# Sixty-four unread bytes behind the attention's output: every feed-forward tile starts 64 bytes later

## The chip, the cores and the metric

One core of one Trainium2 chip runs the whole program. The metric is the device time of one execution in microseconds (us). It is given as the median of three runs, and one more execution was recorded by the hardware profiler.

## What is computed

A decaying linear attention is followed by two feed-forward layers, on 4 x 768 = 3,072 tokens of 256 channels. Cut to what matters:

```python
# attention, per batch and head (8 heads of 32 channels, 16 states), chunk by chunk
y[:, :, sl] = M @ xc + (Cc @ state) * decay_to_i      # M = (Cc Bc^T) * decays, causal
state = decay_full * state + sum_j(Bc_j x_j * decay_from_j)
# first feed-forward layer, d_ff = 1024
xk = mu_k * x + (1 - mu_k) * x_prev ; xr = mu_r * x + (1 - mu_r) * x_prev
k = max(xk @ w_k, 0) ; r = sigmoid(xr @ w_r) ; x = r * ((k * k) @ w_v)
# second feed-forward layer, d_ff = 2048
h = x @ w_in ; out = (h - tanh(h)) @ w_out
```

## The kernel before, in words

Channels lie on the 128 partitions, in two halves, and tokens run along the free dimension, in 6 blocks of 512. The attention's output and, later, the first layer's output are kept in one tile, `xall`, two halves of `NTOK + 8` float32 a partition. A program written out by hand, and then a planner with due times (`Plan.run`), set the order in which every engine's instructions stand.

Each float32 matrix product is made of three float32r matmuls on TensorE: a number is split into a high and a low part, and weight-high x data-high, weight-low x data-high and weight-high x data-low are added in PSUM. The function `product` (L755, L756, L758) does this for the products whose sums go up (into `pk`, `pr` in the first layer, `ph` in the second), and `down_part` (L765, L766, L767) for those that go down into `acc`. Every one of these matmuls has a 128x128 weight block, 512 contiguous bytes a partition, and streams 512 columns of data, 2,048 contiguous bytes a partition. Before each there is a weight load of its own (LDWEIGHTS).

A block of the first layer takes 108 such matmuls, 648 in all. The second layer is cut into 48 units (6 blocks, j, times 8 slices of 256 hidden channels, i); a unit takes 12 matmuls up and 12 down. Between the two ScalarE squares the result twice (`poly_a`, L884 and L885), VectorE finishes a polynomial for h - tanh(h) (L889, L893), one of the two copies the high part (L352 or L354), and VectorE makes the low part (L902). Six buffers serve in turn: `xh` and `xl` hold a block's data, `h` and `l` a unit's result, both streamed by TensorE; `f` and `s` are for ScalarE and VectorE.

Where the tiles stand follows from the order in which pools are opened. From the low end of each partition come the constants, `xall` (pool `zp`), the buffers `f h s l xh xl` (pool `work`), the second layer's weights of units i = 0 and 1 (pool `w2e`) and all weights of the first layer (pool `w1p`). From the high end comes a right-hand side: the attention's tiles (pool `att`), and after it, in the same place, the second layer's weights of units i = 2 to 7 (pool `w2p`) and the output buffers `ob`. In the built program, in bytes of each partition:

| tiles | start before | modulo 128 | start after | modulo 128 |
|---|---|---|---|---|
| `xall`, first half | 2,912 | 96 | 2,912 | 96 |
| `xall`, second half | 15,232 | 0 | 15,264 | 32 |
| `f h s l xh xl` (4,096 bytes each) | 27,552 and on | 32 | 27,616 and on | 96 |
| `winh winl wouth woutl`, i = 0, 1 (2,048 each) | 88,992 and on | 32 | 89,056 and on | 96 |
| `wkh wkl wrh wrl wvh wvl` | 105,376 and on | 32 | 105,440 and on | 96 |
| attention's `sr` (weights of `pd`), `rr` (its data) | 163,808 and 164,832 | 96 | the same | 96 |
| `winh winl wouth woutl`, i = 2 to 7 | 159,712 and on | 96 | the same | 96 |

All tiles of the first four kinds that TensorE reads have lengths that are multiples of 512 bytes, so that a weight block or a half of a data tile has the remainder of its tile. The matmul of L428, whose result is `pd`, is one of the attention's: 116 rows of weights from `sr`, 512 columns of `rr`, two in a row, placed between matmuls of the first layer.

Of the kernel before, what the change touches and what calls it, by code (L numbers as in the profile page):

```python
# [7 lines left out]
F32 = mybir.dt.float32  # L8
# [8 lines left out]
P = 128  # L17
# [3 lines left out]
NTOK = NB * S  # L21
# [174 lines left out]
def chain_kernel(ctx, tc, xb, a, an, a0, bc, mu_k, mu_r, w_k, w_v, w_r, w_in, w_out, out):  # L196
# [7 lines left out]
    zp = ctx.enter_context(tc.tile_pool(name="zp", bufs=1))  # L204
# [37 lines left out]

    xall = zp.tile([P, 2, NTOK + 8], F32, name="xall")

    def col(t):
        return t + t // S
# [856 lines left out]
```

## Time and profile before

| | |
|---|---|
| median of 3 runs | 507.31 us (507.01 to 508.74) |
| the profiled execution | 507.41 us, its span 505.7 us |
| TensorE busy | 482.5 us, 95% of the span |
| TensorE weight loads | 382.3 us, 76% |
| VectorE busy | 401.4 us, 79% |
| ScalarE busy | 293.1 us, 58% |
| mean granted TensorE clock | 0.978 |

The span runs from the first to the last instruction. TensorE's matmuls overlap in the profile and their ends are modelled, so that the busy share says that it always had one in flight, not how fast they followed each other; that is read from their starts.

### The profile page before, as it was taken

Reading aid. Unit: us, or ns where it says so; the run is one execution under the profiler, and the core shown is the slowest. Engines: PE = TensorE matmul, PEld = TensorE weight load, DVE = VectorE, ACT = ScalarE, POOL = GpSimd, SP = SyncE. Lnnn points to the kernel's source line nnn. Section 1 sums busy time; section 2 is a strip of 40 time slices with the busy share of each in tenths; the row PEclk is TensorE's granted clock in tenths of the full one; section 3 lists DMA queues with packets and bytes.
Section 4 is the critical chain, followed back from the end, with each engine's and each line's share of the span. In section 5 each row is a group of like instructions: output and inputs, shape, how many; then the busy total and the mean of one; then the engine's idle time right before and its main releaser. Section 6 shows DMA issues by size and latency. Waiting matters only on the chain.

```text
span 505.7 us, 10270 instructions
## 1 busy us (share of the span) xinstructions
PE 482.5 (95%) x4462; PEld 382.3 (76%) x4462; DVE 401.4 (79%) x509; ACT 293.1 (58%) x374; POOL 6.1 (1%) x22
## 2 busy tenths in 40 slices
PE   5979989999999999999999999999999999999993
PEld 2557767888778878877788788788878888887882
DVE  6698998999669999996877868767876966787581
ACT  5366976775757666766464654645565454455551
POOL 4000000000000000000000000000000000000000
PEclk9789999999999999999999999999999999999998
DMA  6575455211022212210000100100010010001001
GB/s 196 183 231 181 136 156 152 76 47 34 1 86 84 83 43 84 83 43 0 1 0 1 41 0 1 41 3 0 1 41 0 1 41 1 0 1 41 0 2 47
DMA packets 14259, 27.40 MB, mean 54 GB/s; under 512 B 2392, under 2 KB 3288, under 8 KB 14208
## 3 DMA queue, kind: packets, MB, share of 16 engines
q1 hardware_dynamic: 14140, 26.66, 16.9%
q8 instruction: 37, 0.61, 0.5%
q14 instruction: 14, 0.11, 0.1%
q10 hardware_dynamic: 68, 0.02, 0.0%
HBM read 23.30 MB, written 3.34 MB: 53 GB/s over the span
## 4 chain that ended last, share of the span: by engine, by line
PE 69%; DVE 18%; ACT 6%; DMA 3%; issue 2%; ACTq 0%; POOL 0%; DVEq 0%; POOLq 0%; SPq 0%
PE acc L765 10%; PE acc L767 10%; PE acc L766 10%; PE ph L755 8%; PE ph L758 8%; PE ph L756 8%; PE pk L755 3%; PE pk L756 2%; PE pk L758 2%; DVE l L788 2%; DVE f L889 2%; DVE f L893 1%; DMA raw<-in_w_in 1%; PE py L504 1%; PE py L482 1%
## 5 line engine op out<-in xcount | busy, mean ns | idle before, releaser
L884 ACT ACTIVATE s<-ph 128x1024 f32<-128x1024 f32 (+1 forms) x49 | 49.4, 1009 | 76.3 <-PE ph L758 76.3
L889 DVE SCALAR_TENSOR_TENSOR f<-f,s 128x1024 f32<-128x1024 f32 (+1 forms) x49 | 58.8, 1200 | 34.8 <-ACT f L885 34.4
L755 PE MATMUL ph<-xh,winh 128*128 128x512 f32 x192 | 76.2, 397 | 0.0
L756 PE MATMUL ph<-xh,winl 128*128 128x512 f32 x192 | 75.5, 393 | 0.0
L765 PE MATMUL acc<-h,wouth 128*128 128x512 f32 x188 | 74.5, 396 | 0.2
L767 PE MATMUL acc<-l,wouth 128*128 128x512 f32 x188 | 74.5, 396 | 0.1
L766 PE MATMUL acc<-h,woutl 128*128 128x512 f32 x188 | 74.3, 395 | 0.0
L902 DVE TENSOR_TENSOR l<-f,h 128x1024 fp32r<-128x1024 f32 (+1 forms) x49 | 58.9, 1201 | 18.6 <-ACT h L352 18.0
L352 ACT ACTIVATE h<-f 128x1024 fp32r<-128x1024 f32 (+1 forms) x43 | 44.7, 1039 | 48.5 <-DVE f L893 45.6
L893 DVE TENSOR_TENSOR f<-ph,f 128x1024 f32<-128x1024 f32 (+1 forms) x49 | 58.9, 1201 | 3.3
L758 PE MATMUL ph<-xl,winh 128*128 128x512 f32 x192 | 60.2, 395 | 0.0
L885 ACT ACTIVATE f<-s,biases 128x1024 f32<-128x1024 f32 (+1 forms) x49 | 55.6, 1136 | 1.6
L765 PEld LDWEIGHTS acc<-h,wouth 128*128 128x128 f32 x188 | 35.4, 188 | 10.0 <-ACT f L885 1.4
L755 PEld LDWEIGHTS ph<-xh,winh 128*128 128x128 f32 x192 | 36.1, 188 | 8.8
L758 PEld LDWEIGHTS ph<-xl,winh 128*128 128x128 f32 x192 | 36.1, 188 | 8.6
L767 PEld LDWEIGHTS acc<-l,wouth 128*128 128x128 f32 x188 | 35.4, 188 | 9.2 <-DVE l L902 1.0
L756 PEld LDWEIGHTS ph<-xh,winl 128*128 128x128 f32 x192 | 36.1, 188 | 8.1
L766 PEld LDWEIGHTS acc<-h,woutl 128*128 128x128 f32 x188 | 35.4, 188 | 8.2
L755 PE MATMUL pk<-xh,wkh 128*128 128x512 f32 x96 | 39.3, 409 | 0.0
L765 PE MATMUL acc<-h,wvh 128*128 128x512 f32 x96 | 38.5, 401 | 0.9 <-DVE xall L817 0.9
L756 PE MATMUL pk<-xh,wkl 128*128 128x512 f32 x96 | 38.2, 398 | 0.0
L767 PE MATMUL acc<-l,wvh 128*128 128x512 f32 x96 | 37.6, 392 | 0.3 <-DVE l L788 0.3
(138 smaller groups left out, 754.0 us busy)
## 6 DMA issues: line engine op xcount, KB each, us to landing
bct<-in_bc SPq DMA_DIRECT2D x12, 384.0 KB
xbt<-in_xb SPq DMA_DIRECT2D x12, 384.0 KB
raw<-in_w_in SPq DMA_DIRECT2D x8, 512.0 KB
raw<-in_w_out SPq DMA_DIRECT2D x8, 512.0 KB
out<-ob SPq DMA_DIRECT2D x11, 256.0 KB
raw<-in_w_k SPq DMA_DIRECT2D x4, 512.0 KB
raw<-in_w_v SPq DMA_DIRECT2D x4, 512.0 KB
raw<-in_w_r SPq DMA_DIRECT2D x1, 512.0 KB
```

What stands on the lines that cost most here:

```text
L352: A.activation(out=out, in_=in_, func=AF.Copy)
L755: PE.matmul(o, wh[:, k, ms], hi[:, k], start=k == 0, stop=False)
L756: PE.matmul(o, wl[:, k, ms], hi[:, k], start=False, stop=False)
L758: PE.matmul(o, wh[:, k, ms], lo[:, k], start=False, stop=k == 1)
L765: PE.matmul(acc[:, c], wh[:, k, cs], h[:, e], start=first, stop=False, skip_group_check=True)
L766: PE.matmul(acc[:, c], wl[:, k, cs], h[:, e], start=False, stop=False, skip_group_check=True)
L767: PE.matmul(acc[:, c], wh[:, k, cs], l[:, e], start=False, stop=last, skip_group_check=True)
L884: A.activation(out=s, in_=phs[j, i][:, e], func=AF.Square, accum_out=sums[:, c:c + 1])
L885: A.activation(out=qs[j, i][:, e], in_=s, func=AF.Square, scale=PA, bias=pbias)
L889: V.scalar_tensor_tensor(out=q, in0=q, scalar=PG, in1=s, op0=ALU.add, op1=ALU.mult)
L893: V.tensor_tensor(out=q, in0=phs[j, i][:, e], in1=q, op=ALU.mult)
L902: V.tensor_tensor(out=l[:, e], in0=qs[j, i][:, e], in1=f(h[:, e]), op=ALU.subtract)
```

## The change

The tile `xall` gets 16 columns more than tokens in each half in place of 8. Nothing reads or writes the new columns.

```diff
-    xall = zp.tile([P, 2, NTOK + 8], F32, name="xall")
+    xall = zp.tile([P, 2, NTOK + 16], F32, name="xall")
```

The tile grows by 2 x 8 x 4 = 64 bytes a partition. Its second half moves by 32 bytes, and all that is allocated after it from the low end moves by 64, as in the table. The right-hand side stays where it was. Every engine's instructions are the same, in the same order; only addresses differ.

## Rows read from the trace of the kernel before

**Rows 1.** The page: shares by engine of the chain of work that ended last.

```profile
PE 69%; DVE 18%; ACT 6%; DMA 3%; issue 2%; ACTq 0%; POOL 0%; DVEq 0%; POOLq 0%; SPq 0%
```

**Rows 2.** The chain that ended last, in order of time: start, length, what.

```profile
474.06 0.48 PE ph L758 x2
474.57 1.12 ACT s L884 x2
...
495.19 3.02 PE acc L972 x18
```

**Rows 3.** The waits that began from 242 to 474 us: total, times, longest.

```profile
ACT s L884 <- PE ph L758: 67.0, 40, 3.3
...
PEld acc L765 <- ACT f L885: 1.4, 3, 0.5
```

**Rows 4.** TensorE in order of time, first layer: start, length, line, tiles.

```profile
191.18 0.39 PE L755 MATMUL pk<-xh,wkh 128*128 128x512 f32 x1
...
193.90 0.39 PE L755 MATMUL pk<-xh,wkh 128*128 128x512 f32 x1
```

**Rows 5.** The same view, second layer, units i = 3 to 7 of j = 1.

```profile
299.14 0.40 PE L755 MATMUL ph<-xh,winh 128*128 128x512 f32 x1
...
303.34 0.40 PE L765 MATMUL acc<-h,wouth 128*128 128x512 f32 x1
...
304.74 0.40 PE L755 MATMUL ph<-xh,winh 128*128 128x512 f32 x1
```

**Rows 6.** Stretches side by side: TensorE busy (instructions), granted clock, DMA share, GB/s.

```profile
145.00:223.00 78.00, 77.14 (x344) 1.00 0.27 82
242.00:474.00 232.00, 231.77 (x993) 1.00 0.03 12
```

**Rows 7.** The same for all engines: PE, PEld, DVE, ACT, POOL, then clock.

```profile
190.00:218.00 28.00, 28.00 (x125) 23.10 (x125) 27.26 (x39) 20.57 (x24) 0.00 (x0) 1.00 0.31 93
300.00:328.00 28.00, 28.00 (x122) 22.51 (x121) 22.92 (x23) 14.50 (x20) 0.00 (x0) 1.00 0.05 19
```

**Rows 8.** TensorE in order of time, j = 5: units i = 0 between others.

```profile
445.96 0.39 PE L767 MATMUL acc<-l,wouth 128*128 128x512 f32 x1
...
447.58 0.39 PE L755 MATMUL ph<-xh,winh 128*128 128x512 f32 x1
...
448.94 0.40 PE L765 MATMUL acc<-h,wouth 128*128 128x512 f32 x1
...
450.33 0.39 PE L755 MATMUL ph<-xh,winh 128*128 128x512 f32 x1
```

**Rows 9.** Weight loads in order of time, beside the matmuls of Rows 5.

```profile
303.34 0.19 PEld L766 LDWEIGHTS acc<-h,woutl 128*128 128x128 f32 x1
```

**Rows 10.** TensorE in order of time around two pairs of `pd`.

```profile
61.07 0.62 PE L428 MATMUL pd<-rr,sr 116*128 116x512 f32 x2
61.52 0.39 PE L755 MATMUL pr<-xh,wrh 128*128 128x512 f32 x1
...
105.37 0.62 PE L428 MATMUL pd<-rr,sr 116*128 116x512 f32 x2
105.82 0.39 PE L765 MATMUL acc<-h,wvh 128*128 128x512 f32 x1
```

**Rows 11.** TensorE in order of time where block 5 takes over `acc`.

```profile
459.64 0.63 PE L758 MATMUL ph<-xl,winh 128*128 128x512 f32 x2
...
460.65 0.39 PE L766 MATMUL acc<-h,woutl 128*128 128x512 f32 x1
```

**Rows 12.** Two lines that read both halves of `xall`: ns min/median/max.

```profile
L775 ACT ACTIVATE f<-xall,muk x12: 711/716/723, 34.6 to 182.2; 128x512 f32<-128x512 f32 x12
...
L780 DVE SCALAR_TENSOR_TENSOR f<-xall,omk,f x12: 743/746/751, 35.4 to 184.9; 128x512 f32<-128x512 f32 x12
```

**Rows 13.** VectorE's writes into weight tiles, by line: busy, mean ns of one.

```profile
L329 DVE TENSOR_TENSOR winl<-keep,winh 128x512 fp32r<-128x512 f32 x8 | 5.5, 686 | 0.1
L329 DVE TENSOR_TENSOR wkl<-keep,wkh 128x512 fp32r<-128x512 f32 x4 | 2.7, 687 | 0.9 <-ACT wkh L352 0.9
```

## The prediction

> **What bounds the kernel now.** The question is whether 64 bytes of address can matter at all, so the views are read in this order: the chain that ended last, to see whose speed sets the end; the waits, to see whether that engine is held up by others; and then the starts of its instructions, to see what its speed depends on.
>
> The chain lies on TensorE for 69% of the span [rows 1]. In the second layer it stays there from 242 to 474 us; the last 31 us belong to ScalarE and VectorE, which work off the last units, and TensorE's last 18 matmuls [rows 2]. In those 232 us ScalarE waits 67.0 us for TensorE, while the largest of the waits of TensorE's weight loads is 1.4 us in all [rows 3]. So from 242 to 474 us a nanosecond saved on a matmul is a nanosecond of the end, and elsewhere only in part.
>
> The starts tell the speed. In the first layer 12 matmuls start between 191.18 and 193.90: 2.72 us / 12 = 226.7 ns each [rows 4]. In the second layer 24 start between 299.14 and 304.74: 5.60 / 24 = 233.3 ns [rows 5]. The matmuls are of one form, 128x128 by 512 columns of float32r, and both stretches have the full granted clock, 1.00 [rows 6, 7]. The other engines are not the reason either: VectorE is busy 27.26 of 28 us where the matmuls are fast, and 22.92 of 28 where they are slow; ScalarE 20.57 and 14.50 [rows 7].
>
> What differs is the address. In the first layer data and weights both start at 32 modulo 128 (the table of tiles). In rows 5 the data start at 32 and the weights, of units i = 3 to 7, at 96. The second layer has its own test of this, since units i = 0 and 1 have weights at 32. In block 5 unit 0 comes up between units whose weights are at 96: from 445.96 to 447.58 seven matmuls take 1.62 / 7 = 231.4 ns, the next six, to 448.94, take 1.36 / 6 = 226.7 ns, and the six that follow, with weights at 96 again, 1.39 / 6 = 231.7 ns [rows 8]. Within 5 us, with the same clock and the same company, the slow pace goes when the remainders agree and comes back when they do not. That it takes some matmuls to settle suggests a phase: the weights of a matmul are read while the data of the one before stream (the load for L766 starts at 303.34 with the matmul of L765, and ends 0.19 us later [rows 5, 9]), and the two reads get out of each other's way only if their lines agree. This is a conjecture; the pace is what is measured.
>
> **The change, part by part.** No instruction is added, removed or moved.
>
> *Data tiles and first-layer weights go from 32 to 96 together.* Their distance stays a multiple of 128 (of 512, even). If distance counts, the first layer keeps its 226.7 ns. The trace has one matmul with both operands at 96: `pd`. Its pairs stand among first-layer matmuls, and where these are settled the pair takes 0.45 us, from 61.07 to 61.52 and from 105.37 to 105.82, so 225 ns each [rows 10]. That is the fast pace, with weights at 96. It has 116 rows instead of 128, and a pair is short, so this speaks for the distance without proving it.
>
> *Second-layer weights of units 2 to 7 stay at 96, and the data come to them.* Distance 64 becomes 0. The price of a matmul afterwards is bounded by the two paces of the trace, 226.7 below and 233.3 above; I take 226.7, since rows 4, 8 and 10 all show it wherever the remainders agree. Between 242 and 474 us there are 993 matmuls [rows 6]: 993 x 226.7 ns = 225.1 us in place of 232.0. From the difference of 6.9 us come off the halts of TensorE that remain, where a block's `acc` is waited for: the three matmuls from 459.64 to 460.65 take 1.01 us in place of 0.70, 0.31 us lost [rows 11]. There are three like this and some smaller ones, 1.0 us by my estimate. A halt waits for ScalarE's copy while TensorE has less to do meanwhile, so each of the five block ends grows by about 6 matmuls x 6.6 ns = 0.04 us, 0.2 us. After each some matmuls are unsettled again, 7 x (231.4 - 226.7) ns = 0.03 us [rows 8], 0.2 us in all. 6.9 - 1.0 - 0.2 - 0.2 = 5.5 us.
>
> *Before 242 and after 474 us* I count nothing: there ScalarE, VectorE and their transfers hold the chain. That the attention's `pd`, now at the same remainder as its neighbours, disturbs them less could give up to 0.5 us; it widens the range only.
>
> *Does the faster TensorE run into another engine?* A unit takes 24 x 233.3 = 5.60 us now and would take 5.44. ScalarE waits 67.0 us for TensorE in 232 us [rows 3], 28 us per 100, so it can follow a pace that is 2.8% faster. What is late next is the low part `l` (L902), for which the weight load of L767 waits; TensorE has waited little for it so far, and it would have some 0.25 us less (an estimate: about 40 matmuls x 6.6 ns lie between the release of ScalarE's first square and that load).
>
> *`xall`'s second half moves from 0 to 32 modulo 128; every buffer and first-layer weight tile of ScalarE and VectorE moves too.* L775 and L780 read both halves, which stand 32 apart modulo 128, in 711 to 723 and 743 to 751 ns [rows 12]; L329 writes `wkl` at 32 in 687 ns and `winl`, mostly at 96, in 686 [rows 13]. Those engines do not care: 0 us. If they did by the whole spread of rows 12, 1%, it would be hidden where TensorE bounds.
>
> A rule of the Trainium skill speaks against all this. "SBUF — State Buffer", section "Who interferes with whom", gives TensorE two independent read ports, one for the moving operand and one for LDWEIGHTS, and says that PE and ACT never wait on anyone. By that, no address would change the pace and the sum would be 0 us. The trace does not agree: 226.7 and 233.3 ns in rows 4, 5 and 8 with nothing else changed.
>
> Sum: -5.5 us on the profiled execution's 507.41 us (its span, 505.7, and 1.7 around it, which stays) gives **501.9 us**. That execution is 0.1 us above the median shown, 507.31, which the range covers.
>
> **The rivals.**
>
> *The weights' own address counts (slower).* If a weight block at 96 is slow by itself, whatever the data's address, the change makes slow what was fast. The first layer's 648 matmuls lose 6.6 ns each, of which the 344 from 145 to 223 us [rows 6] fully (2.3 us), and the 304 before, where the attention is interleaved, between nothing and all (up to 2.0 us). In the second layer units 0 and 1 lose about 233.3 - 229.2 (13 matmuls of rows 8 in 2.98 us) = 4 ns on some 250 matmuls, 1.0 us. Sum +3.3 to +5.3, middle 511.7 us. For it: in rows 4, 5 and 8 a weight at 96 always goes with 233 ns, since the data never moved. Against it: `pd` [rows 10]. The point that decides is the first layer's pace: above about 229 ns with all at 96, this is it.
>
> *The remainder is not the cause (no change), 507.4 us.* The weights that go with 233.3 ns also lie above byte 157,000 of the partition, those with 226.7 below 142,240 (105,376 + 4 x 8,192 + 2 x 2,048); it could be the region, which the change leaves alone. For it: rows 5 and 8 cannot tell the two apart. Against it: `pd`'s weights lie at 163,808 and take 225 ns [rows 10], but so do its data. By the Trainium skill, "SBUF — State Buffer", section "Who interferes with whom", it would end here too, since no read of TensorE would wait for another.
>
> *TensorE gets faster, but ScalarE and VectorE take the bound (part of the gain), about 504.5 us.* Half of the gain is left if the pace stays unsettled near 230 ns or if the low part comes too late. Against it are the 67.0 us of ScalarE's waits [rows 3].
>
> **How the numbers follow.** Forecast 0.70, weights' own address 0.15, no change 0.11, part of the gain 0.04. A measurement of this kernel tells about 0.3%, 1.5 us, from no change. Faster by more than that: 0.70 + 0.04 = 0.74; within it 0.11; slower 0.15. The forecast's own range is 500.9 (0.5 us from `pd`, 0.5 for the scatter of runs) to 503.5. To leave out no more than 2 in 10 the range takes in the partial gain and no change, up to 507.8; the slower case is left out.
>
> **What would show it.** Right: 24 matmuls of units 2 to 7 in about 5.44 us, first-layer pace still 226.7, ScalarE and VectorE durations unchanged, a second layer about 5.5 us shorter with the stretch before 223 us as it was. Wrong by the first rival: first-layer groups of 12 in 2.80 us. Wrong by the second: both paces as before. Wrong in size: new waits of TensorE for L902 or L352 behind the 1.4 us of rows 3, or a pace between 227 and 233.

## The result, and the profile after

The changed kernel takes 500.75 us (median of 4 runs, 499.31 to 501.83), the kernel before 507.16 in the same measurement. The ratio is 0.9895, with a 95% interval of 0.9863 to 0.9928: 5.3 us less (3.7 to 6.9); the two medians, of four runs each, lie 6.4 us apart. The profiled execution took 501.83 us, its span is 500.0 us, 5.7 less than before. The forecast was 501.9 us; the median lies 0.15 us under the low end of the range.

TensorE in order of time, first layer and second layer; columns are start, length, engine, line, operation, tiles:

```profile
191.05 0.39 PE L755 MATMUL pk<-xh,wkh 128*128 128x512 f32 x1
...
193.77 0.39 PE L755 MATMUL pk<-xh,wkh 128*128 128x512 f32 x1
...
293.59 0.39 PE L765 MATMUL acc<-h,wouth 128*128 128x512 f32 x1
...
299.03 0.39 PE L765 MATMUL acc<-h,wouth 128*128 128x512 f32 x1
```

In the first layer 12 matmuls take 2.72 us as before [rows 4]. In the second layer 24 take 5.44 us, 226.7 ns each, where they took 5.60 [rows 5]. Both layers now go at one pace, and the first layer's did not suffer from its new place.

The number of TensorE instructions in the stretch that the forecast used (busy us, count, granted clock, DMA share, GB/s), after:

```profile
242.00:474.00 232.00, 231.66 (x1018) 1.00 0.03 12
```

25 more matmuls fit into the same 232 us than before [rows 6]. The chain that ended last, after, shows what this does to the end:

```profile
468.40 0.47 PE ph L758 x2
...
468.89 1.12 ACT s L884 x2
...
489.50 3.03 PE acc L972 x18
```

The hand-over from TensorE to ScalarE that stood at 474.57 us [rows 2] stands at 468.89, 5.68 us earlier, and what follows is as long as before: 505.7 - 474.57 = 31.1 us, 500.0 - 468.89 = 31.1 us. All the gain lies ahead of this point. Before the second layer nothing moved in these two executions: its first matmul (L755 into `ph`) starts at 223.8 us before and 223.7 after. So the gain arose in the second layer.

The waits that began from 242 to 468 us, after (total, times, longest):

```profile
ACT s L884 <- PE ph L758: 59.7, 40, 3.1
...
PEld acc L765 <- ACT f L885: 1.5, 3, 0.5
PEld acc L767 <- DVE l L902: 0.6, 1, 0.6
```

TensorE still waits for next to nothing, and ScalarE still waits for it most of all [rows 3]. The halt at a block's end grew a little, as the rows around block 5 show:

```profile
454.26 0.62 PE L758 MATMUL ph<-xl,winh 128*128 128x512 f32 x2
...
455.30 0.39 PE L766 MATMUL acc<-h,woutl 128*128 128x512 f32 x1
```

Three matmuls take 1.04 us there, 1.01 before [rows 11]: 0.36 us lost in place of 0.31. The second layer has eight start-to-start intervals over 262 ns, at five block ends; against 226.7 ns each they lost 1.06 us before and 1.26 after. ScalarE and VectorE kept their durations; the lines that read both halves of `xall`, and the writes into weight tiles, after (busy us, mean ns of one, idle before):

```profile
L780 DVE SCALAR_TENSOR_TENSOR f<-xall,omk,f 128x512 f32<-128x512 f32 x12 | 8.5, 747 | 0.0
...
L775 ACT ACTIVATE f<-xall,muk 128x512 f32<-128x512 f32 x12 | 8.0, 722 | 0.0
...
L329 DVE TENSOR_TENSOR winl<-keep,winh 128x512 fp32r<-128x512 f32 x8 | 5.5, 684 | 0.1
L329 DVE TENSOR_TENSOR wkl<-keep,wkh 128x512 fp32r<-128x512 f32 x4 | 2.7, 687 | 2.4 <-ACT wkh L352 2.4
```

747 ns against a median of 746, 722 against 716 [rows 12], 684 and 687 against 686 and 687 [rows 13].

### The profile page after: what moved, and what is told of

The parts are those of the page before. It is cut to its first block, busy times and chain, and to the rows that moved or that the text cites. A ratio compares the mean times of both kernels' runs of the same rounds, so it can differ in the third digit from the quotient of the medians.

```text
span 500.0 us, 10270 instructions
## 1 busy us (share of the span) xinstructions
PE 473.2 (95%) x4462; PEld 380.0 (76%) x4462; DVE 400.9 (80%) x509; ACT 292.8 (59%) x374; POOL 6.3 (1%) x22
## 4 chain that ended last, share of the span: by engine, by line
PE 69%; DVE 18%; ACT 7%; issue 2%; DMA 2%; ACTq 0%; POOL 0%; DVEq 0%; POOLq 0%
PE acc L765 10%; PE acc L767 10%; PE acc L766 10%; PE ph L755 8%; PE ph L756 8%; PE ph L758 8%; PE pk L755 3%; PE pk L756 2%; PE pk L758 2%; DVE l L788 2%; DVE f L889 2%; DVE f L893 2%; DMA raw<-in_w_in 1%; PE py L482 1%; PE py L504 1%
## 5 line engine op out<-in xcount | busy, mean ns | idle before, releaser
L755 PE MATMUL ph<-xh,winh 128*128 128x512 f32 x192 | 74.8, 389 | 0.0
L756 PE MATMUL ph<-xh,winl 128*128 128x512 f32 x192 | 74.7, 389 | 0.0
L765 PE MATMUL acc<-h,wouth 128*128 128x512 f32 x188 | 73.6, 392 | 0.3
L767 PE MATMUL acc<-l,wouth 128*128 128x512 f32 x188 | 73.5, 391 | 0.3 <-DVE l L902 0.2
L766 PE MATMUL acc<-h,woutl 128*128 128x512 f32 x188 | 73.2, 389 | 0.0
L758 PE MATMUL ph<-xl,winh 128*128 128x512 f32 x192 | 59.1, 389 | 0.0
L765 PEld LDWEIGHTS acc<-h,wouth 128*128 128x128 f32 x188 | 35.3, 188 | 9.0 <-ACT f L885 1.5
L755 PEld LDWEIGHTS ph<-xh,winh 128*128 128x128 f32 x192 | 36.1, 188 | 7.5
L758 PEld LDWEIGHTS ph<-xl,winh 128*128 128x128 f32 x192 | 36.0, 188 | 7.5
L767 PEld LDWEIGHTS acc<-l,wouth 128*128 128x128 f32 x188 | 35.3, 188 | 8.5 <-DVE l L902 1.1
L756 PEld LDWEIGHTS ph<-xh,winl 128*128 128x128 f32 x192 | 36.1, 188 | 7.5
L766 PEld LDWEIGHTS acc<-h,woutl 128*128 128x128 f32 x188 | 35.3, 188 | 7.2
L765 PE MATMUL acc<-h,wvh 128*128 128x512 f32 x96 | 38.4, 400 | 0.9 <-DVE xall L817 0.9
L755 PE MATMUL pk<-xh,wkh 128*128 128x512 f32 x96 | 39.1, 407 | 0.0
L756 PE MATMUL pk<-xh,wkl 128*128 128x512 f32 x96 | 37.9, 395 | 0.0
L767 PE MATMUL acc<-l,wvh 128*128 128x512 f32 x96 | 37.6, 392 | 0.3 <-DVE l L788 0.3
```

The source lines that it names most:

```text
L755: PE.matmul(o, wh[:, k, ms], hi[:, k], start=k == 0, stop=False)
L756: PE.matmul(o, wl[:, k, ms], hi[:, k], start=False, stop=False)
L758: PE.matmul(o, wh[:, k, ms], lo[:, k], start=False, stop=k == 1)
L765: PE.matmul(acc[:, c], wh[:, k, cs], h[:, e], start=first, stop=False, skip_group_check=True)
L766: PE.matmul(acc[:, c], wl[:, k, cs], h[:, e], start=False, stop=False, skip_group_check=True)
L767: PE.matmul(acc[:, c], wh[:, k, cs], l[:, e], start=False, stop=last, skip_group_check=True)
```

## The experiments

The theory going in: a matmul's pace depends on the distance between where its weights and its data start, and the distance counts modulo 128. The main rivals: the weights' or the data's own start counts, or what moved in ScalarE's and VectorE's buffers, or the free space itself. The programs of all experiments have the same instructions in the same order; only addresses differ. Two numbers are read from each trace beside the time. The pace is the mean of the 848 start-to-start intervals under 262 ns that begin with a matmul of units 2 to 7 (longer ones are halts); where a text on record gives it for a kernel already measured, its figure can be 0.1 ns higher than here. The second layer's length runs from the first way down of unit 2 (L765) to the last matmul of the last way up (L758); it was 247.2 to 488.1 us before, 241.0 us when worked out from unrounded starts, and 247.0 to 482.1 after, 235.1 us.

**Move the other side instead.** Nothing on the low end moves; the attention's tiles and the weights of units 2 to 7 come down by 64 bytes, to 32 modulo 128:

```diff
+    ctx.enter_context(tc.tile_pool(name="padp", bufs=1, side="right")).tile([P, 16], F32, name="pad")
     att = att_stack.enter_context(tc.tile_pool(name="att", bufs=1, side="right"))
```

> The kernel before, with an unused tile of 64 bytes at the high end, so that the attention's tiles and the second layer's weights of units 2 to 7 move down by 64 bytes and start at 32 modulo 128; xall, all buffers and the other weights stay at 32 as they were. Distance theory (what counts is the distance modulo 128 between data and weights): every matmul at 226.7 ns, 24 matmuls of the second layer in 5.44 us, time as with the change, 500.8 us (499.5 to 502). Rival, the data's own start counts (96 is good): data stay at 32, 24 matmuls in 5.60 us, 507.2 us. Rival, what the moved buffers of ScalarE and VectorE or xall's second half do: none of them moves, 507.2 us.

Measured: 500.84 us, ratio 0.9889 (0.9848 to 0.9930). The pace is 226.7 ns, the second layer 235.1 us long, to a tenth what the change gave. TensorE's instructions from 250 to 466 us:

```profile
250.00:466.00 216.00, 215.66 (x948) 1.00 0.04 13
```

The changed kernel has 949 there. The data, `xall` and all buffers stand here as before the change, so none of them made the gain, and 96 is no better a start than 32. What counts is that weights and data agree.

**Agree modulo what?** `xall` 128 bytes longer (NTOK + 24, shown) and 192 bytes longer (NTOK + 32):

```diff
-    xall = zp.tile([P, 2, NTOK + 8], F32, name="xall")
+    xall = zp.tile([P, 2, NTOK + 24], F32, name="xall")
```

> The kernel before with xall 128 bytes longer in place of 64 (NTOK + 24): everything from the low end moves by 128 bytes and starts at 32 modulo 128 again, as before the change. Distance theory: 24 matmuls of units 2 to 7 in 5.60 us, 507.2 us (506 to 508.5). Rival, that the tile is longer or that there is free space between tiles: 500.8 us as with the change, or lower.

Measured: 501.18 us, ratio 0.9908 (0.9880 to 0.9937). A miss for the theory as it stood: with 128 bytes more every tile has the remainder modulo 128 that it had before, and most of the gain is there all the same.

> xall 192 bytes longer (NTOK + 32): data and low weights start at 96 modulo 128, as with the change, but at 96 modulo 256, where the weights of units 2 to 7 are at 224 modulo 256. Distance theory with a period of 128 bytes: 24 matmuls in 5.44 us, 500.8 us (499.5 to 502). Distance theory with a period of 256 bytes or more: 24 matmuls in 5.60 us in units 2 to 7, 507.2 us.

Measured: 504.06 us, ratio 0.9968 (0.9943 to 0.9993). With 192 bytes more every feed-forward tile starts at 96 modulo 128, as after the change, and hardly a third of the gain is there; in the second layer's length it is a fifth (239.8 us). The two in order of time, 128 bytes more first:

```profile
293.30 0.39 PE L765 MATMUL acc<-h,wouth 128*128 128x512 f32 x1
...
298.79 0.39 PE L765 MATMUL acc<-h,wouth 128*128 128x512 f32 x1
```

192 bytes more:

```profile
299.68 0.40 PE L765 MATMUL acc<-h,wouth 128*128 128x512 f32 x1
...
305.26 0.39 PE L765 MATMUL acc<-h,wouth 128*128 128x512 f32 x1
```

24 matmuls take 5.49 us in the one (228.8 ns) and 5.58 in the other (232.5 ns). So 128 is not the period. In the first layer, where weights and data keep a distance that is a multiple of 512 in all these kernels, the pace is the same in each, 227.7 to 227.9 ns in the mean of its intervals under 262 ns: the free space does nothing by itself.

**The period.** `xall` 320 bytes longer (NTOK + 48) and 256 bytes longer (NTOK + 40), distances of -256 and -192 bytes:

> The runs with 128 and 192 bytes more showed that a period of 128 bytes is wrong: units 2 to 7 went at 229.0 ns at a distance (weights minus data) of -64 bytes and at 232.5 at -128, against 233.3 at +64. Here xall is 320 bytes longer (NTOK + 48), a distance of -256 bytes. Distance theory with a period of 256: units 2 to 7 at 226.7 ns, second layer as with the change, about 5 us under the kernel before. Distance theory with a period of 512: another pace, 229 to 233.4 ns, up to 3.5 us under the kernel before.

Measured: 500.69 us, ratio 0.9881 (0.9834 to 0.9928), pace 226.7 ns, second layer 235.1 us.

> xall 256 bytes longer (NTOK + 40), a distance of -192 bytes, which is +64 modulo 256. Period of 256: units 2 to 7 at 233.3 ns, 24 matmuls in 5.60 us, the time of the kernel before. Period of 512: a pace of its own, not necessarily 233.3.

Measured: 505.60 us, ratio 0.9996 (0.9970 to 1.0022), pace 233.2 ns, second layer 241.0 us, as before the change. -256 is as good as 0, and -192 as bad as +64, while 64 and 128 bytes did not bring the pace back: of the steps tried, 256 bytes is the period.

**The places between.** `xall` 32, 96, 160 and 224 bytes longer (NTOK + 12, + 20, + 28, + 36):

> xall 32 bytes longer (NTOK + 12): data and low weights start at 64 modulo 128, the weights of units 2 to 7 at 96, a distance of 32 bytes. Distance theory with lines of 64 bytes, of which half collide: a pace between 226.7 and 233.3 ns in units 2 to 7, about 230, 504 us. Distance theory where any distance but 0 is bad: 507.2 us. Rival, the data's own start counts: some other pace in the first layer too, where data and weights agree and the distance theory expects 226.7 ns.

> xall 96 bytes longer (NTOK + 20): data and low weights start at 0 modulo 128, the weights of units 2 to 7 at 96, a distance of -32 bytes (weights 32 bytes behind a multiple of 128 in the other direction than with 32 bytes more). Distance theory, symmetric: the same pace in units 2 to 7 as with 32 bytes more; first layer 226.7 ns. Rival, the data's own start counts: 0 modulo 128 is as good a start as any, 226.7 ns everywhere, 500.8 us.

> xall 160 bytes longer (NTOK + 28), a distance of -96 bytes (+160 modulo 256), between -64 (229.0 ns) and -128 (232.5 ns). If the pace falls off smoothly with the distance from 0: about 231 ns in units 2 to 7. If only -64 is special: 232.5 to 233.4 ns. First layer, at distance 0: 227.8 ns in the mean as in all runs.

> xall 224 bytes longer (NTOK + 36), a distance of -160 bytes (+96 modulo 256), between +64 (233.3 ns) and +128 (232.5 ns). With a period of 256 bytes and 0 as the only good place: 232.5 to 233.4 ns in units 2 to 7, the time of the kernel before.

Measured, with the others, by the distance from data to weights modulo 256 (weights of units 2 to 7 start at 224 modulo 256 in all but the first experiment):

| distance, bytes | kernel | pace, ns | second layer, us | ratio to the kernel before (95%) |
|---|---|---|---|---|
| 0 | the change (+64 bytes) | 226.7 | 235.1 | 0.9895 (0.9863 to 0.9928) |
| 0 | +320 bytes | 226.7 | 235.1 | 0.9881 (0.9834 to 0.9928) |
| 0 | right-hand side -64 | 226.7 | 235.1 | 0.9889 (0.9848 to 0.9930) |
| +32 | +32 bytes | 232.9 | 240.4 | 1.0009 (0.9981 to 1.0038) |
| +64 | before | 233.2 | 241.0 | 1 |
| +64 | +256 bytes | 233.2 | 241.0 | 0.9996 (0.9970 to 1.0022) |
| +96 | +224 bytes | 233.8 | 241.1 | 1.0031 (1.0002 to 1.0060) |
| 128 | +192 bytes | 232.4 | 239.8 | 0.9968 (0.9943 to 0.9993) |
| -96 | +160 bytes | 233.3 | 241.0 | 1.0013 (0.9995 to 1.0031) |
| -64 | +128 bytes | 228.9 | 236.8 | 0.9908 (0.9880 to 0.9937) |
| -32 | +96 bytes | 233.3 | 241.0 | 1.0021 (0.9997 to 1.0045) |

No smooth curve: 0 is the one good place, -64 is two thirds of the way to it, all others lie within 1.5 ns of each other. The guess of half a collision at 32 bytes was a miss, and so was the smooth fall for -96. That +32 and -32 are equally bad holds, as do the first layers at data starts of 0, 32, 64, 96, 128, 160, 192 and 224 modulo 256: all between 227.7 and 227.9 ns, where the distance is 0.

**What the first layer would lose.** 64 unused bytes between the buffers and the weights, in the kernel before and in the changed one:

```diff
+    w2e.tile([P, 16], F32, name="pad")
     for _ in range(NE):
         unit_weights(w2e)
```

> The kernel before with 64 unused bytes behind the buffers: data stay at 32 modulo 128, and all weights of both layers start at 96. Distance theory and the rival of the weights' own address agree here: first layer at 233.3 ns too (12 matmuls in 2.80 us), units 0 and 1 too, 510.7 to 512.7 us, 511.7 as worked out for that rival. It measures the price of the first layer.

Measured: 508.02 us against 505.77 for the kernel before in the same measurement, ratio 1.0044 (1.0017 to 1.0070): 2.2 us more. The direction was right and the size a miss, half of what was expected. The pace of the first layer is 233.3 ns as expected, 12 matmuls in 2.80 us (in order of time, columns as above):

```profile
191.74 0.39 PE L765 MATMUL acc<-h,wvh 128*128 128x512 f32 x1
...
194.54 0.39 PE L765 MATMUL acc<-h,wvh 128*128 128x512 f32 x1
```

From the attention's last matmul (L504) to the second layer's first one the kernel before takes 223.8 - 144.8 = 79.0 us, this one 223.9 - 143.9 = 80.0. So the first layer's slower pace costs 1.0 us of the 2.3 that its matmuls lose. Most of the rest went into a halt. The kernel before has one in this stretch, where TensorE waits for VectorE (in brackets: idle time, and what ended it):

```profile
185.50 0.61 PE L758 MATMUL pk<-xl,wkh 128*128 128x512 f32 x2
186.98 0.47 PE L765 MATMUL acc<-h,wvh 128*128 128x512 f32 x1 [0.86 <-DVE xall L817]
```

With all weights apart TensorE comes there later and does not halt:

```profile
185.68 0.63 PE L758 MATMUL pk<-xl,wkh 128*128 128x512 f32 x2
186.14 0.39 PE L765 MATMUL acc<-h,wvh 128*128 128x512 f32 x1
```

The intervals over 262 ns of this stretch lost 1.2 us before and 0.1 here. The second layer, where units 0 and 1 are at a distance too, takes 241.6 - 241.0 = 0.6 us more. The remaining 0.6 of the 2.2 us are not traced; the scatter of the runs is larger.

> The changed kernel with 64 unused bytes behind the buffers: data at 96, the weights of the first layer and of units 0 and 1 at 32, those of units 2 to 7 at 96. Distance theory: first layer at 233.3 ns, units 0 and 1 near 231 ns, units 2 to 7 at 226.7 ns, so 2.3 to 4.3 us for the first layer and about 1.0 us for units 0 and 1 on top of 500.8 us: 504.1 to 506.1 us. Rival, the weights' own address counts: weights at 32 are good and weights at 96 bad, first layer 226.7 ns, units 2 to 7 233.3 ns, 507.2 us. Rival, the data's own start counts (96 is good): 226.7 ns everywhere, 500.8 us.

Measured: 503.99 us, ratio 0.9966 (0.9942 to 0.9990), 3.2 us over the changed kernel's median of the earlier measurement; just under the expected range. First layer 233.3 ns, units 0 and 1 at 232.5, units 2 to 7 at 228.1. In the profiled executions the first layer is 1.0 us longer than with the change (80.0 us, counted as above), the second 2.4 (237.5 us), more than the 1.0 expected. This settles the rivals of an own address: weights at 32 are the slower ones here and weights at 96 the faster, the reverse of before the change, with data at 96. That units 2 to 7 do not reach 226.7 is the cost of their neighbours: after a matmul at a distance several others need to settle, and those that follow at least six others at distance 0 without a halt go at 227.1.

**Whose distance counts.** The changed kernel, with the weights of units 2 to 7 allocated so that the low parts alone (`winl`, `woutl`) are at +64 (lines shortened where dots stand):

```diff
-            for _ in range(NE, NP2):
-                unit_weights(w2p)
+            for part in "hl":
+                for i, (nm, shape) in [...]: w2[nm + part].append(w2p.tile(shape, F32R, ...))
+                w2p.tile([P, dict(h=16, l=112)[part]], F32, name="pad" + part)
```

> The changed kernel with the weights of units 2 to 7 allocated high parts first: winh and wouth at distance 0 of the data, winl and woutl at +64 bytes (modulo 512). Only the matmuls of L756 and L766 have weights at a distance. If the read of the next matmul's weights disturbs the streaming of the data, the matmul before them (L755, L765) lasts longer from start to start; if a matmul's own weights count, L756 and L766 do. Mean pace between 226.7 and 233.3 ns, about 229 ns if a third of the matmuls bear the whole cost, and 1 to 2 us over the changed kernel.

Measured: 502.54 us, ratio 0.9936 (0.9904 to 0.9968), pace 229.9 ns, where about 229 was expected; second layer 237.7 us, 2.6 longer than with the change. In order of time:

```profile
300.61 0.39 PE L765 MATMUL acc<-h,wouth 128*128 128x512 f32 x1
300.84 0.40 PE L766 MATMUL acc<-h,woutl 128*128 128x512 f32 x1
301.07 0.39 PE L767 MATMUL acc<-l,wouth 128*128 128x512 f32 x1
301.30 0.39 PE L765 MATMUL acc<-h,wouth 128*128 128x512 f32 x1
301.53 0.40 PE L766 MATMUL acc<-h,woutl 128*128 128x512 f32 x1
301.77 0.39 PE L767 MATMUL acc<-l,wouth 128*128 128x512 f32 x1
302.00 0.39 PE L755 MATMUL ph<-xh,winh 128*128 128x512 f32 x1
```

The starts have steps of 10 ns here; in the mean of 140 each, the interval from L765 to L766 is 227.5 ns and from L766 to L767 235.8 ns. So on the way down, by the recorded starts, the matmul with the distant weights itself bears the cost, not the one during which these weights are loaded. On the way up the first L756 of a pair is the same (235.5 ns, 72 times), but the second, with the same weight tile, is not (226.8 ns to the following L758, 72 times), while the L755 before both are somewhat longer (229.9). A rule in which the matmul's own weights always cost does not fit either. Nor is a load recorded as slower: the loads of units 2 to 7 last 188.2 ns in the mean in the kernel before and 187.7 in the changed one. What shrank is the time from the end of a load to the start of its matmul, from 42.4 to 35.7 ns.

## Why the prediction was right, and where it was not

**TensorE bounds from 242 to 474 us, and a nanosecond there is one of the end: shown.** The gain stands complete at the hand-over, 5.68 us, and the 31.1 us behind it are unchanged.

**The distance between data and weights sets the pace: shown.** Moving either side gave the same (ratios 0.9895 and 0.9889, pace 226.7 ns in both), and with the low weights moved apart in the changed kernel the two layers changed roles. Both rivals of that kind, the weights' own address and the place above byte 157,000, fall: the weights above it went at 226.7 ns without having moved.

**226.7 ns as the price of a matmul, 5.5 us as the sum: shown.** 993 matmuls in 232 us became 1,018. The span fell by 5.7 us and the ratio says 5.3. In the second layer the 1,023 intervals under 262 ns went from 232.7 to 226.8 ns, 6.1 us, and the halts grew by 0.2 us, as forecast: 5.9 us.

**The median of 500.75 us, below the range, comes of the base and of scatter, not of the gain.** The forecast took 5.5 us off one execution of 507.41 us. In the later measurements the kernel before gave medians of 505.05 to 505.77 us in 15 to 25 runs each, so that the first four runs (median 507.16) were high, while the three kernels at distance 0 have medians of 500.69 to 500.84. With that base the forecast would have been near 500. Part of the scatter lies ahead of the second layer: in the profiled executions of this study the attention's last matmul starts anywhere from 141.5 to 146.3 us, with nothing in the attention's instructions changed. That it started at 144.8 and 144.7 us in the two that are compared above is luck.

**The step that failed: "the two reads get out of each other's way only if their lines agree", agreement taken modulo 128.** The condition was too weak. That the forecast came out is luck here: the change happened to bring the distance to 0 modulo 512, and the argument from `pd` had the same luck: `sr` and `rr` both start at 224 modulo 256. The runs with 128 and 192 bytes more showed that 128 is not the period, and those with 256 and 320 that 256 is. A pad chosen by the remainder modulo 128 would have hit or missed by chance. The conjecture behind it, that the load of the next weights disturbs the data that stream meanwhile, was not supported: with only the low parts apart, the interval in which they are loaded took 227.5 ns on the way down and 229.9 on the way up, and the large growth, to 235.5 to 235.8, stood in the interval behind it. What in TensorE or its memory makes the delay stays open; these runs show where it appears, not why.

**The rival's price was too high.** Weights apart in the first layer were put at 3.3 to 5.3 us more; the experiment gave 2.2. The 344 matmuls from 145 to 223 us were counted as bounding "fully", although TensorE's halt there stood in the rows (busy 77.14 of 78.00 us [rows 6]); 1.1 of the 2.3 us lost went into that halt. Units 0 and 1 cost 0.6 us in place of 1.0.

**ScalarE and VectorE do not feel the move: shown** by their durations, and by the first experiment, in which nothing of theirs on the low end moved.

By the Trainium skill, "SBUF — State Buffer", section "Who interferes with whom", TensorE's two read ports are independent, and by that no address would count. These traces do not agree: the table of distances shows 226.7 to 233.8 ns.

## What to carry to other kernels

Where TensorE bounds, work out the pace of one matmul form from its starts in each stretch; if two stretches with the same form and the same granted clock differ, compare the start addresses of weights and data. For float32r matmuls of 512 columns, each with its own weight load, put weight and data tiles at the same remainder modulo 256 (other forms were not tried): a pad on either side does it, and it was worth 2.8% of TensorE's time wherever that was the bound. A comparison inside the trace (units whose weights lay elsewhere) finds such an effect without a run, but it cannot tell the period; that takes two or three pads.

## What the hardware showed that was not expected

A matmul's pace depends on the distance between weights and data with a period of 256 bytes, and not smoothly: 226.7 ns at 0, 228.9 at -64, 232.4 to 233.8 at 128, ±96, ±32 and +64. Distances of opposite sign are not equal: +64 gives 233.2 and -64 gives 228.9 ns. The pace also has a memory: after a halt, or after matmuls at a distance, some three to nine matmuls at distance 0 (mostly five or six) still take 223 to 237 ns before they settle at 226 or 227.
